# Attention with sinks and a window, then two expert layers: loads, masks and two queues put in a written order

## The chip, the cores and the metric

The kernel runs on one core of one Trainium2 chip. The time is the device time of one execution in microseconds, median of several runs. The engines of the core work side by side, each through its own list of instructions: PE (TensorE), DVE (VectorE), ACT (ScalarE), POOL (GpSimd) and SP (SyncE, which here only issues transfers and holds a queue of its own).

## The reference

Two batches of 8 heads, 768 positions, head size 64. Each position attends to the first `n_sink` = 4 positions and to the last `window` = 128. The result goes to a layer of 8 experts (each token to one of them, by the largest gate logit), and then through a dense layer with the activation h * tanh(softplus(h)).

```python
scores = (q @ k.T) / sqrt(64)
keep   = (pos_k < n_sink) | ((0 <= pos_q - pos_k) & (pos_q - pos_k < window))
a      = softmax(where(keep, scores, -1e9))
x      = (a @ v)                       # 1536 tokens x 512
e      = argmax(x @ w_gate)            # one expert for each token
y      = gate * sigmoid(x @ w_output_gate)[e] * (relu(x @ w1[e]) @ w2[e])
h      = y @ w_in
out    = (h * tanh(softplus(h))) @ w_out
```

`n_sink` and `window` are inputs of the kernel (64-bit integers on the device), and so are the weights w_in and w_out (64-bit floats, read as pairs of 32-bit words and narrowed on the chip).

## The kernel before

There are two forms of attention. `fast()` holds for sinks up to 16 and windows up to 129, which these inputs fulfil; `general()` holds for all others and is not executed here, though its instructions lie in the program between the opening part and the fast form. Every engine reads a flag (`values_load`, L800) and branches (L801).

The opening part loads the two parameters, k and q of the pairs 0 and 1, and prepares constants: masks `m0`, `m1` and `m2` on GpSimd (L194 to L206), which then loads the first 16 rows of v of all heads into `vsr` (L211).

The fast form works on pairs of heads, 8 in all (4 for each batch). A loop over `g` (L641) runs the stages of several pairs in each turn: the scores of pair g, the preparation (transposes of k and q) of pair g + 1, the transposes of the probabilities of pair g - 1, and the product with v and the tail of pair g - 2. In a turn the string in `SEQS` names the order of the parts: p is a quarter of the preparation, s the scores of one block of 128 queries for both heads, a the transposes of the probabilities, v the product, t the tail (transposes back, logits of the gates), m and n copies of the sink columns and the sums, r a part of the routing of a batch whose pairs are done, u a part of the narrowing of w_in. PE keeps this order in any case (`tc.issue_after`). The lists of DVE, ACT, POOL and SP are ordered by a planner, which takes first what it holds to be ready, so the order on them isn't that of the source.

Transfers of a turn, after its parts: `load_kq(g + 3)` (k and q in halves, 8 transfers of 96 KB), `load_v(g + 1)` (2 of 192 KB), one piece of the first expert's weights (512 KB), one or two fills of `table` with zeros (384 KB each, the first 640 KB). QK has two sets of buffers, so a k or q half can only be loaded when the transposes of the pair two before have read it.

Narrowing of w_in: a piece `nr` of 512 KB is loaded (`load_in`, L308), scaled (L294 on GpSimd for pieces below 5, L291 on DVE for others), put together in three steps on DVE (L285, L286, L287) and stored to `wi32` (L318, 256 KB); the store's part also asks for the piece after the next. Seven pieces are done here, piece u in turn u + 2. The loads of the first two pieces stand at the end of turn 0 in the source.

Scores (L547, L549): DVE adds the mask, takes the maximum and frees one of 4 PSUM buffers; ACT makes the exponentials. `kT` is copied by DVE (L510), `qT` by ACT (L512), the sink columns of kT by DVE (L516) for the pairs 0 and 1 and by POOL for others. The product's two banks are copied by DVE (L624, L627); they share 4 PSUM buffers `pt` with all transposes.

Routing (turn 6 for the first batch, turn 10 for the second): `choose` finds the expert of each token, `rank` counts ranks on PE and DVE and gives the row of each token in `table`, and also the factor `gsc` from the gates by way of an exponential `ez` on ACT (L442, L448, L450, L452); `place` scales the rows (L393) and scatters them (L394).

Of the kernel before, what the change touches and what calls it, by code (L numbers as in the profile page):

```python
# [47 lines left out]
def tile_kernel(  # L48
# [21 lines left out]
    keeps = dram.tile([S, S], F32, name="keeps")  # L70
# [32 lines left out]
    def load_kq(g, engs=(nc.sync, nc.sync)):  # L103
        for h in range(2):
            for t, src, eng in zip(QK[g % 2][h], (k, q), engs):
                load_rows(t, src, g, h * LT_, LT_, eng)
# [4 lines left out]
    load_kq(0, (nc.sync, nc.scalar))  # L111
    load_kq(1)
# [26 lines left out]
    ns, wd = pv[:, 0:1], pv[:, 1:2]  # L139
    wx = mid.tile([P, NP, 2, 2 * E], F32, name="wx")  # L140
# [53 lines left out]
    with tc.manual_schedule(engines={ET.Pool}):  # L194
        wdm = mid.tile([P, 1], F32, name="wdm")
# [206 lines left out]
    def route_units(b, sb, pst):  # L402
# [22 lines left out]
        def rank():  # L425
# [36 lines left out]
        def rank_(b=b):  # L462
# [6 lines left out]
        return [choose, rank_] + ([lambda i=i: place(b, 2 * i, 2) for i in range(3)] if b == 0 else [])  # L469
# [15 lines left out]


    def fast():
# [147 lines left out]

        prep0 = prep_units(0)
        for u in prep0[:2]:
            u()
        late, after, tail, routing, prod = [], [], [], [], []
        steps_ = [lambda: None]  # L640
        for g in range(NG + 3):  # L641
# [15 lines left out]
            if g == 0:  # L657
                lane["0"] = [prep0[2], lambda: (prep0[3](), load_kq(2), load_v(0), load_wx())]
# [19 lines left out]
            if g == 0:  # L678
                for u in range(2):
                    load_in(u, nra)  # L680
# [6 lines left out]
            for e in {1: (0,), 2: (1, 2), 3: (3, 4), 4: (5, 6), 5: (7,)}.get(g, ()):  # L687
                zero_fill(e)
        st.close()


    def general():
# [11 lines left out]
        for u in range(2):  # L704
            load_in(u, nra)
        for u in range(NF_):
            for x_ in narrow_in(u, nra, qkv):
                x_()
        rel = cb.tile([P, S], F32, name="grel")
        sk = cb.tile([P, S], F32, name="gsk")  # L710
        nc.gpsimd.iota(rel, [[1, S]], base=0, channel_multiplier=0, allow_small_or_imprecise_dtypes=True)
        nc.vector.tensor_scalar(sk, rel, ns, None, ALU.is_lt)
        g0 = cb.tile([P, S], F32, name="gg0")
        gk = cb.tile([P, S], F32, name="ggk")
        for i in range(NB):
            nc.gpsimd.iota(rel, [[-1, S]], base=i * P, channel_multiplier=1, allow_small_or_imprecise_dtypes=True)
            nc.vector.tensor_scalar(g0, rel, 0.0, None, ALU.is_ge)
            nc.vector.scalar_tensor_tensor(g0, rel, wd, g0, ALU.is_lt, ALU.mult)
            nc.vector.tensor_tensor(gk, g0, sk, ALU.max)
            nc.sync.dma_start(out=keeps[i * P:(i + 1) * P, :], in_=gk)  # L720
# [15 lines left out]
        with tc.For_i(0, B, 1) as b_, tc.For_i(0, NP, 1) as hp, tc.For_i(0, NB, 1) as i:  # L736
            row = b_ * (H * S) + hp * (2 * S)
            for j in range(2):
                cs = slice(j * D, (j + 1) * D)
                nc.sync.dma_start(out=qr[:, cs], in_=qf[ds(row + i * P + j * S, P), :])  # L740
                for t, src in ((kr, kf), (vr, vf)):
                    nc.sync.dma_start(out=t[:, :, cs], in_=src[ds(row + j * S, S), :].rearrange("(i p) d -> p i d", p=P))
                for c_, w_ in ((0, w_gate), (E, w_og)):
                    nc.sync.dma_start(out=wl[cs, j, c_:c_ + E], in_=w_[ds(hp * P + j * D, D), :])
            nc.sync.dma_start(out=keep, in_=keeps[ds(i * P, P), :])
# [4 lines left out]
            for i0 in (0, 3):  # L750
                pt = psT.tile([P, 512], F32, name="pt")
                for a in range(3):
                    nc.tensor.transpose(pt[:, a * P:(a + 1) * P], kr[:, i0 + a], ident)
                nc.scalar.activation(kT[:, i0 * P:(i0 + 3) * P], pt[:, 0:3 * P], AF.Copy)
# [28 lines left out]
            nc.sync.dma_start(out=parts[ds(b_ * (NP * S) + hp * S + i * P, P), :], in_=xo)  # L783
# [832 lines left out]
```

## Time and profile before

| | |
|---|---|
| median of 3 runs | 586.36 us (586.34 to 587.57) |
| the profiled execution | 586.35 us, of which its span 584.7 us |
| PE busy | 557.9 us, 95% of the span |
| DVE busy | 309.2 us, 53% |
| ACT busy | 348.2 us, 60% |
| POOL busy | 46.5 us, 8% |
| DMA | 79.32 MB, mean 136 GB/s |

The span runs from the first instruction to the last. Attention takes about the first 131 us of it, a first chunk of expert 0 goes to 151, the experts go on to 314, and the dense layer fills the rest. A busy share is a mean over stages with different limits.

### The profile page before, as it was taken

How to read it: one execution, taken by the hardware profiler on the slowest of the kernel's cores; microseconds unless marked ns; L12 is line 12 of the kernel's file. 1: busy time of each engine (PE TensorE's matmuls, PEld its weight loads, DVE VectorE, ACT ScalarE, POOL GpSimd, SP SyncE). 2: the span in 40 equal slices, each digit the busy share in tenths (PEclk: the TensorE clock that was granted, in tenths of full speed). 3: DMA queues.
4: the chain of work that ended last, by engine and by line, in shares of the span. 5: the costliest groups of instructions: out<-in, count | busy, mean ns of one | idle time of the engine just before them, and what ended most of it. 6: DMA issues, size and time to landing. Idle time of an engine off the chain costs nothing.

```text
span 584.7 us, 9722 instructions
## 1 busy us (share of the span) xinstructions
PE 557.9 (95%) x3568; PEld 487.5 (83%) x3568; DVE 309.2 (53%) x743; ACT 348.2 (60%) x668; POOL 46.5 (8%) x95
## 2 busy tenths in 40 slices
PE   3859998999999999999999999999999999999995
PEld 2648777789999999999999888888888888888884
DVE  3645788864142036788977996866313233213112
ACT  2837787731111145764546988879767668667572
POOL 8020113204000000000000000000200000200002
PEclk9979999999999999999999999999999999999998
DMA  6697997704999962995421333220100000100002
GB/s 123 145 250 208 235 235 254 242 21 170 377 369 368 324 222 74 399 306 170 126 73 34 102 105 121 72 74 0 73 0 1 0 2 1 73 0 1 0 1 76
DMA packets 72669, 79.32 MB, mean 136 GB/s; under 512 B 42112, under 2 KB 52352, under 8 KB 72608
## 3 DMA queue, kind: packets, MB, share of 16 engines
q1 hardware_dynamic: 68688, 71.61, 40.4%
q0 software_dynamic: 2176, 6.56, 3.0%
q8 instruction: 31, 0.51, 0.4%
q10 hardware_dynamic: 1744, 0.39, 0.4%
q14 instruction: 30, 0.25, 0.1%
HBM read 66.23 MB, written 12.32 MB: 134 GB/s over the span
## 4 chain that ended last, share of the span: by engine, by line
PE 77%; issue 14%; ACT 3%; DMA 2%; DVE 2%; POOL 1%; SPq 0%; POOLq 0%; DVEq 0%; ACTq 0%
PE h L1380 16%; PE acc L1397 15%; PE Y L1067 6%; PE h L1057 6%; PE pt L360 5%; PE Y L1018 5%; PE pt L363 5%; PE h L1000 5%; PE s L363 4%; PE h L1003 3%; ACT p L549 2%; PE Y L1020 2%; PE Y L857 2%; PE h L363 2%; DMA nr<-in_moe_w_in_dram 1%
## 5 line engine op out<-in xcount | busy, mean ns | idle before, releaser
L1429 DVE TENSOR_TENSOR fx<-h,fx 128x512 f32<-128x512 f32 x48 | 30.9, 685 | 127.2 <-ACT fx L1426 127.2
L1420 ACT ACTIVATE fx<-h,nln 128x512 f32<-128x512 f32 x48 | 32.7, 689 | 52.5 <-PE h L1380 52.1
L549 ACT ACTIVATE p<-ms,nm 128x272 f32<-128x272 f32 (+1 forms) x96 | 47.0, 491 | 20.8 <-DVE nm L547 20.8
L1018 PE MATMUL Y<-hs,wch 128*128 128x384 f32 (+1 forms) x160 | 45.3, 355 | 0.0
L1411 POOL DMA_INDIRECT out_dram<-nr,idx x12 | 11.6, 970 | 417.5 <-DVE nr L1407 414.8
L1060 ACT ACTIVATE t<-h 128x256 f32<-128x256 f32 x20 | 7.7, 383 | 58.7 <-PE h L1057 55.0
L547 DVE CUSTOM_DVE_ANT_0 ms<-s,m 128x272 f32<-128x272 f32 (+1 forms) x96 | 34.5, 409 | 11.7 <-ACT ph L579 5.8
L1020 PE MATMUL Y<-hs,wcl 128*128 128x192 f32 (+1 forms) x160 | 39.2, 245 | 0.0
L363 PE MATMUL s<-kT,qT 64*128 64x272 f32 (+1 forms) x192 | 30.2, 418 | 9.2 <-DVE nm L547 6.3
L1380 PE MATMUL h<-yh,wah 128*128 128x512 f32 x96 | 37.5, 391 | 0.0
L1380 PE MATMUL h<-yh,wal 128*128 128x512 f32 x96 | 37.4, 389 | 0.0
L1397 PE MATMUL acc<-wdh,gh 128*128 128x512 f32 x96 | 37.4, 389 | 0.0
L1397 PE MATMUL acc<-wdl,gh 128*128 128x512 f32 x96 | 37.4, 389 | 0.0
L1433 ACT ACTIVATE gh<-fx 128x512 fp32r<-128x512 f32 x48 | 29.5, 633 | 7.2 <-DVE fx L1429 7.2
L1437 DVE TENSOR_TENSOR gl<-fx,gh 128x512 fp32r<-128x512 f32 x48 | 31.0, 688 | 2.4
L1420 ACT ACT_TABLE_LOAD x24 | 30.8, 1283 | 0.4
L1426 ACT ACT_TABLE_LOAD x24 | 30.8, 1283 | 0.4
L1020 PEld LDWEIGHTS Y<-hs,wcl 128*128 128x128 f32 x160 | 30.6, 191 | 0.0
L363 PEld LDWEIGHTS s<-kT,qT 64*128 64x128 f32 x192 | 17.4, 198 | 15.5 <-DVE nm L547 7.3
L1018 PEld LDWEIGHTS Y<-hs,wch 128*128 128x128 f32 x160 | 30.1, 188 | 0.1
L1426 ACT ACTIVATE fx<-fx 128x512 f32<-128x512 f32 x48 | 27.7, 625 | 0.3
L1397 PE MATMUL acc<-wdh,gl 128*128 128x512 f32 x96 | 27.7, 390 | 0.0
(297 smaller groups left out, 1397.6 us busy)
## 6 DMA issues: line engine op xcount, KB each, us to landing
raw<-in_moe_w_dram SPq DMA_DIRECT2D x24, 512.0 KB, 6.6
rbx<-in_moe_w_dram SPq DMA_DIRECT2D x24, 512.0 KB, 6.8
rax<-in_moe_w_dram SPq DMA_DIRECT2D x16, 512.0 KB, 8.3
nr<-in_moe_w_out_dram SPq DMA_DIRECT2D x16, 512.0 KB, 3.8
nr<-in_moe_w_in_dram SPq DMA_DIRECT2D x13, 512.0 KB, 6.4
vr<-in_v_dram SPq DMA_DIRECT2D x16, 192.0 KB, 3.4
table<-zer SPq DMA_DIRECT2D x7, 384.0 KB, 6.6
rax<-wi SPq DMA_DIRECT2D x5, 512.0 KB, 8.4
```

Source lines behind the costliest of these rows:

```text
L363: last_pe[0] = nc.tensor.matmul(*args, **kw)
L547: nc.vector.tensor_tensor_reduce(ms[:, 0:w], s[j][:, 0:w], m, 1.0, 3.0e38, ALU.add, ALU.min, nm[:, j, i:i + 1])
L549: nc.scalar.activation(p[:, j, i, o:o + w], ms[:, 0:w], AF.Exp, bias=nm[:, j, i:i + 1], scale=-1.0, accum_out=sm[:, j, i:i + 1])
L1018: nc.tensor.matmul(Y[c // 2][:, c % 2, 0:2 * w], lhsT=wh, rhs=hT[b][:, f].rearrange("p s c -> p (s c)"), start=(b == 0 and f == 0), stop=F ...
L1020: nc.tensor.matmul(Y[c // 2][:, c % 2, 0:w], lhsT=wl, rhs=hT[b][:, f, 0], start=False, stop=(b == 3 and f == 1), skip_group_check=True)
L1057: nc.tensor.matmul(hp[:, f, 0:P], lhsT=w_[:, d, f * P:(f + 1) * P], rhs=XT[:, d], start=(d == 0), stop=(d == NP - 1), skip_group_check=True)
L1067: nc.tensor.matmul(Y[c // 2][:, c % 2, 0:P], lhsT=raw_[4 + b][:, f * 512 + c * P:f * 512 + (c + 1) * P], rhs=hT[b][:, f, 0:P], start=(b == ...
L1380: mm = nc.tensor.matmul(h, lhsT=wt[:, (fb % 8) * P:(fb % 8 + 1) * P], rhs=xx[d], start=(k_ == 0), stop=(k_ == 11))
L1397: nc.tensor.matmul(accs[tb], lhsT=g_[:, tb * P:(tb + 1) * P], rhs=w_[:, c], start=(fb == 0 and k_ == 0), stop=(fb == NF - 1 and k_ == 2))
L1420: st[n]["sg"] = nc.scalar.activation(x_, st[n]["h"], AF.Sigmoid, bias=nln2)
L1426: nc.scalar.activation(st[n]["x"], st[n]["x"], AF.Sin, scale=2.0)
L1437: nc.vector.tensor_tensor(gl, st[n]["x"], st[n]["gh"].bitcast(F32), ALU.subtract)
```

## The change

In the fast form: SP and DVE are put in source order (`manual_schedule` over the loop). The q halves of pair 1's first part are loaded by ScalarE. The two first loads of w_in move from the end of turn 0 into its part 0, behind `load_kq(2)` and ahead of `load_v(0)`; `load_wx` (four small loads of gate weights) moves the other way, to the end of turn 0. The five operations that make `m1` and `m2` go from GpSimd to DVE, behind the first quarter of the preparation, and `wdm` is made by DVE in the opening part. In `rank` the three operations on `ez` and `se` become a part `weigh`: for the first batch it runs with the first `place`, for the second it stands in one block ahead of `rowf`.

In the general form: one loop over pairs and one over blocks in place of three nested loops, keys and values loaded once for a pair, masks made inside, the gate weights joined in `gates`, and w_in narrowed in larger pieces.

```diff
-    load_kq(0, (nc.sync, nc.scalar))
-    load_kq(1)
+    load_kq(0, (0, 1))
+    load_kq(1, (0,))
...
+    wdm = mid.tile([P, 1], F32, name="wdm")
+    nc.vector.tensor_scalar(wdm, wd, -float(P), None, ALU.add)
...
-        v_.tensor_scalar(wdm, wd, -float(P), None, ALU.add)
-        v_.tensor_scalar(m2[:, 0:P], rel, wdm, BIG, ALU.is_ge, ALU.mult)
-        v_.tensor_tensor(m1[:, 0:P], m2[:, 0:P], sk, ALU.mult)
-        v_.memset(m1[:, P:KW], BIG)
-        v_.tensor_copy(m1[:, KW:WIN], m2[:, KW:WIN])
-        v_.tensor_scalar(m2[:, P:KW], sk[:, 0:SC], BIG, None, ALU.mult)
...
-            nc.vector.tensor_scalar(ez, ez, 1.0, None, ALU.add)
+            if b:
+                weigh()
             nc.vector.tensor_reduce(rowf[:, b], rt, AX.X, ALU.add)
-            nc.vector.scalar_tensor_tensor(se, se, 1e-9, ez, ALU.add, ALU.mult)
             nc.vector.tensor_copy(rowi[:, b], rowf[:, b])
-            nc.vector.reciprocal(gsc[:, b], se)
...
+        def weigh():
+            se, ez = d["se"], d["ez"]
+            nc.vector.tensor_scalar(ez, ez, 1.0, None, ALU.add)
+            nc.vector.scalar_tensor_tensor(se, se, 1e-9, ez, ALU.add, ALU.mult)
+            nc.vector.reciprocal(gsc[:, b], se)
...
-        return [choose, rank_] + ([lambda i=i: place(b, 2 * i, 2) for i in range(3)] if b == 0 else [])
+        return [choose, rank_] + ([lambda: (weigh(), place(b, 0, 2))] + [
+            lambda i=i: place(b, 2 * i, 2) for i in (1, 2)] if b == 0 else [])
...
+    def masks():
+        v_ = nc.vector
+        v_.tensor_scalar(m2[:, 0:P], rel, wdm, BIG, ALU.is_ge, ALU.mult)
+        v_.tensor_tensor(m1[:, 0:P], m2[:, 0:P], sk, ALU.mult)
+        v_.memset(m1[:, P:KW], BIG)
+        v_.tensor_copy(m1[:, KW:WIN], m2[:, KW:WIN])
+        v_.tensor_scalar(m2[:, P:KW], sk[:, 0:SC], BIG, None, ALU.mult)
...
+        order = ExitStack()
+        order.enter_context(tc.manual_schedule(engines={ET.SP, ET.DVE}))
         prep0 = prep_units(0)
         for u in prep0[:2]:
             u()
+        masks()
...
-                lane["0"] = [prep0[2], lambda: (prep0[3](), load_kq(2), load_v(0), load_wx())]
+                lane["0"] = [prep0[2], lambda: (prep0[3](), load_kq(2), load_in(0, nra), load_in(1, nra), load_v(0))]
...
             if g == 0:
-                for u in range(2):
-                    load_in(u, nra)
+                load_wx()
```

The loops of the general form, cut to their heads:

```diff
-        with tc.For_i(0, B, 1) as b_, tc.For_i(0, NP, 1) as hp, tc.For_i(0, NB, 1) as i:
...
+        with tc.For_i(0, B * NP, 1) as g:
+            nc.vector.tensor_copy(rel, rel0)
...
+            with tc.For_i(0, NB, 1) as i:
+                block(g, i)
```

## Rows read from the trace of the kernel before

**Rows 1.** Busy time (instructions) by stretch; last columns: clock, DMA share, GB/s

```profile
core 0: us, PE busy (x) PEld busy (x) DVE busy (x) ACT busy (x) POOL busy (x), PEclk, DMA share, GB/s
15.00:28.00 13.00, 11.65 (x86) 8.03 (x82) 9.10 (x44) 11.90 (x42) 0.63 (x3) 1.00 0.66 142
131.00:584.70 453.70, 446.83 (x2623) 400.45 (x2622) 220.56 (x397) 264.49 (x396) 18.01 (x19) 1.00 0.36 120
```

**Rows 2.** Waits of PE, 0 to 131 us: total, times, longest

```profile
PE s L363 <- DVE nm L547: 6.3, 1, 6.3
...
PE s L363 <- DVE kT L510: 2.9, 1, 2.9
PE pt L360 <- DVE xT L624: 1.7, 2, 1.4
...
PE pt L360 <- DMA q0r<-in_q_dram: 0.6, 2, 0.4
```

**Rows 3.** Chain that ended last, 27 to 38 us: start, duration, what

```profile
29.09 5.93 DMA nr<-in_moe_w_in_dram
...
35.09 1.05 POOL nt L294
```

**Rows 4.** Order of time on DVE, 27.8 to 37.4 us: start, duration, instruction, idle before

```profile
36.17 0.43 DVE L285 TENSOR_SCALAR nt<-nt 128x512 int32<-128x512 int32 x1 [7.83 <-POOL nt L294]
...
37.34 0.78 DVE L286 SCALAR_TENSOR_TENSOR nt<-nr,nt 128x512 int32<-128x512 int32 x1
```

**Rows 5.** Busy time by step of one pair, columns as in rows 1

```profile
27.49:49.72 22.23, 15.53 (x114) 11.79 (x113) 11.07 (x39) 11.28 (x37) 3.26 (x4) 0.85 0.85 214
49.72:62.23 12.51, 12.51 (x115) 10.06 (x114) 7.92 (x33) 10.10 (x33) 0.56 (x2) 1.00 0.98 261
62.23:75.20 12.97, 12.73 (x116) 10.05 (x114) 10.22 (x36) 10.21 (x33) 1.57 (x3) 1.00 0.91 233
...
87.99:102.66 14.67, 13.15 (x127) 10.45 (x125) 12.94 (x60) 10.33 (x35) 5.24 (x7) 1.00 0.80 259
102.66:114.26 11.60, 11.60 (x103) 9.20 (x101) 11.28 (x41) 9.23 (x31) 2.95 (x4) 1.00 0.73 215
```

**Rows 6.** Busy time in the stretch of the lower clock, columns as in rows 1

```profile
35.38:42.20 6.82, 5.19 (x26) 3.78 (x28) 5.54 (x19) 3.80 (x13) 2.97 (x4) 0.50 0.94 217
```

**Rows 7.** Order of time on SP: start, duration of the issues, transfer

```profile
9.32 1.02 SPq L94 DMA_DIRECT2D q1r<-in_q_dram  x2
14.15 0.38 SPq L94 DMA_DIRECT2D vr<-in_v_dram  x1
...
29.09 1.01 SPq L308 DMA_DIRECT2D nr<-in_moe_w_in_dram  x2
```

**Rows 8.** DMA issues from 29, from 30.2 and from 22.35: KB, us to landing

```profile
nr<-in_moe_w_in_dram SPq DMA_DIRECT2D x2, 512.0 KB, 6.4
...
k0r<-in_k_dram SPq DMA_DIRECT2D x2, 96.0 KB, 6.5
...
k0r<-in_k_dram SPq DMA_DIRECT2D x2, 96.0 KB, 3.7
```

**Rows 9.** Order of time on DVE, 91.9 to 104.7 us

```profile
93.73 0.17 DVE L448 TENSOR_SCALAR ez<-ez 128x6 f32<-128x6 f32 x1 [1.44 <-ACT ez L442]
...
94.36 0.88 DVE L393 TENSOR_SCALAR xs<-X,gsc 128x512 f32<-128x512 f32 x2
...
98.73 0.43 DVE L547 CUSTOM_DVE_ANT_0 ms<-s,m 128x272 f32<-128x272 f32 x1
...
103.17 0.43 DVE L547 CUSTOM_DVE_ANT_0 ms<-s,m 128x272 f32<-128x272 f32 x1
```

**Rows 10.** Order of time on PE, the product of step 6

```profile
91.55 2.60 PE L363 MATMUL pt<-ph,vr 128*64 128x256 f32 x28
```

**Rows 11.** Order of time on DVE and ACT behind the branch

```profile
9.66 0.56 DVE L510 COPY kT<-pt 128x384 f32<-128x384 f32 x1 [4.37 <-issue]
...
11.28 0.29 DVE L547 CUSTOM_DVE_ANT_0 ms<-s,m 128x128 f32<-128x128 f32 x1 [0.75 <-PE s L363]
...
7.50 0.49 ACT L512 ACTIVATE qT<-pt 128x384 f32<-128x384 f32 x1 [1.69 <-PE pt L360]
```

More of the change, by code (lines that the diff above doesn't have):

```diff
@@ L69, in tile_kernel @@
     table = dram.tile([E * CAP, DM], F32, name="table")
-    keeps = dram.tile([S, S], F32, name="keeps")
+    gates = dram.tile([B * DM, 2 * E], F32, name="gates")
     parts = dram.tile([B * NB * NP * P, 2 * HC], F32, name="parts")
@@ L101, in tile_kernel, with load_kq @@
     HS = [flat[a_] for a_ in range(5)]
-    def load_kq(g, engs=(nc.sync, nc.sync)):
+    def load_kq(g, on_act=()):
         for h in range(2):
-            for t, src, eng in zip(QK[g % 2][h], (k, q), engs):
+            for t, src, eng in zip(QK[g % 2][h], (k, q), (nc.sync, nc.scalar if h in on_act else nc.sync)):
                 load_rows(t, src, g, h * LT_, LT_, eng)
@@ L194, in tile_kernel @@
     with tc.manual_schedule(engines={ET.Pool}):
-        wdm = mid.tile([P, 1], F32, name="wdm")
         v_.tensor_scalar(sk, col, ns, None, ALU.is_ge)
@@ L460, in rank, with rank_ @@
                 nc.vector.tensor_tensor(left, tot, early, ALU.subtract)
-        def rank_(b=b):
+        def weigh():
[3 more added lines that the diff above has]
+            nc.vector.reciprocal(gsc[:, b], se)
+        def rank_():
             if b:
@@ L688, in fast @@
                 zero_fill(e)
+        order.close()
         st.close()
@@ L703, in general @@
             zero_fill(p_)
[L704 to L707, printed above, removed]
-                x_()
-        rel = cb.tile([P, S], F32, name="grel")
+        for b in range(B):
+            for c_, w_ in ((0, w_gate), (E, w_og)):
+                nc.sync.dma_start(out=gates[b * DM:(b + 1) * DM, c_:c_ + E], in_=w_)
+        nar = cb.tile([P, 2048, 2], I32, name="gnar")
+        nat_ = cb.tile([P, 2048], F32, name="gnat")
+        for d in range(2):
+            cut = w_in32[2 * d * P:(2 * d + 2) * P, 0:2048].rearrange("(a p) f -> p a f", p=P)
+            nc.sync.dma_start(out=nar.rearrange("p f w -> p (f w)").rearrange("p (a f) -> p a f", a=2), in_=cut)
+            for x_ in narrow_steps(nat_, nar, scale_dve):
+                x_()
+            nc.sync.dma_start(out=wi32[2 * d * P:(2 * d + 2) * P, 0:1024].rearrange("(a p) f -> p a f", p=P),
+                              in_=nat_.rearrange("p (a f) -> p a f", a=2))
+        rel0 = cb.tile([P, S], F32, name="grel")
         sk = cb.tile([P, S], F32, name="gsk")
[L711 to L720, printed above, removed]
+        nc.gpsimd.iota(rel0, [[1, S]], base=0, channel_multiplier=0, allow_small_or_imprecise_dtypes=True)
+        nc.vector.tensor_scalar(sk, rel0, ns, None, ALU.is_lt)
+        nc.gpsimd.iota(rel0, [[-1, S]], base=-P, channel_multiplier=1, allow_small_or_imprecise_dtypes=True)
+        rel = cb.tile([P, S], F32, name="grl")
         wl = cb.tile([P, 2, 2 * E], F32, name="gwl")
@@ L734, in general, with block @@
         qf, kf, vf = [x_.rearrange("b h s d -> (b h s) d") for x_ in (q, k, v)]
-        with tc.For_i(0, B, 1) as b_, tc.For_i(0, NP, 1) as hp, tc.For_i(0, NB, 1) as i:
-            row = b_ * (H * S) + hp * (2 * S)
+        def block(g, i):
             for j in range(2):
[L739 to L745, printed above, removed]
+                nc.sync.dma_start(out=qr[:, j * D:(j + 1) * D], in_=qf[ds(g * (2 * S) + i * P + j * S, P), :])
+            nc.vector.tensor_scalar(rel, rel, float(P), None, ALU.add)
+            nc.vector.tensor_scalar(km, rel, 0.0, None, ALU.is_ge)
+            nc.vector.scalar_tensor_tensor(km, rel, wd, km, ALU.is_lt, ALU.mult)
+            nc.vector.tensor_tensor(keep, km, sk, ALU.max)
             nc.vector.tensor_scalar(km, keep, BIG, -BIG, ALU.mult, ALU.add)
@@ L749, in general @@
             nc.scalar.activation(qT, pt[:, 0:P], AF.Copy, scale=0.125)
[L750 to L754, printed above, removed]
             for j in range(2):
@@ L782, in general @@
             nc.vector.tensor_copy(xo, pt[:, 0:2 * HC])
-            nc.sync.dma_start(out=parts[ds(b_ * (NP * S) + hp * S + i * P, P), :], in_=xo)
+            nc.sync.dma_start(out=parts[ds(g * S + i * P, P), :], in_=xo)
+        with tc.For_i(0, B * NP, 1) as g:
+            nc.vector.tensor_copy(rel, rel0)
+            for j in range(2):
+                cs = slice(j * D, (j + 1) * D)
+                for t, src in ((kr, kf), (vr, vf)):
+                    nc.sync.dma_start(out=t[:, :, cs],
+                                      in_=src[ds(g * (2 * S) + j * S, S), :].rearrange("(i p) d -> p i d", p=P))
+                nc.sync.dma_start(out=wl[cs, j, :], in_=gates[ds(g * P + j * D, D), :])
+            for i0 in (0, 3):
+                pt = psT.tile([P, 512], F32, name="pt")
+                for a in range(3):
+                    nc.tensor.transpose(pt[:, a * P:(a + 1) * P], kr[:, i0 + a], ident)
+                nc.scalar.activation(kT[:, i0 * P:(i0 + 3) * P], pt[:, 0:3 * P], AF.Copy)
+            with tc.For_i(0, NB, 1) as i:
+                block(g, i)
         for b in range(B):
```

## The prediction

> **What bounds the kernel now.** I read the waits of the matrix engine first, then the chain of waits, then the queues that feed the point it leads to. Only the attention part is touched by what runs: the general form is jumped over with these inputs, so the expert and MLP parts move as a block with the end of attention. From 131 us on PE is busy almost without a gap [rows 1], so a microsecond won or lost before 131 is a microsecond of the total.
>
> PE waits for little in attention: 6.3 us once for DVE's maxima of the scores, 2.9 us once for the first kT copy, 1.7 us in two pieces for the copy of xT [rows 2]. The large one is in the chain [rows 3]: the load of the first w_in piece `nr` lands 5.93 us after its issue, GpSimd scales it (1.05 us), and only then does DVE go on. DVE's own rows [rows 4] show why PE cares: L285, the first DVE step on that piece, stands on DVE ahead of the score rows (L547) of the same pair step, and waits there 7.83 us. PE fills its score buffers and stops.
>
> Cut into steps (a step is a turn of the loop on PE, from its first k transpose to that of the next turn), turn 2, from 27.49 to 49.72, lasts 22.23 us where the next two last 12.51 and 12.97 [rows 5]. Part of it is the clock: the granted clock reads 0.50, the lower of the two levels, over the 6.82 us after the stall, with 5.19 us of PE work in it [rows 6]; at the full level this work takes half, so about 2.6 us. Stall 6.3 and clock 2.6 make 8.9 of the 9.7 us by which the step is longer than the next one.
>
> Why was the piece late? SyncE issued it at 29.09, behind 24 other loads sent from 14.15 on, at about 0.5 us each [rows 7]. The order was the scheduler's.
>
> **The change, part by part.**
>
> *First w_in loads.* In source order SyncE sends, after its jump, the 8 loads of pair 2's k and q, then both `nr` pieces, then v. It also has 2 loads fewer before the jump (two of pair 1's q move to ScalarE). SP's last issue ahead of the jump ended at 10.34, and two issues took 1.02 us there [rows 7], so the jump comes 1 to 2 us earlier and the first load of the fast form goes out between 12.1 and 14.15. Eight issues at 0.5 us put `nr` at 16 to 18.3 instead of 29.09; with the 6.4 us it took to land under load [rows 8] it is there by 22.5 to 24.7. What is pushed behind it, pair 3's k and q, took 3.7 us to land alone and 6.5 us behind `nr` [rows 8]: issued by about 18.5 to 22.5, there by 25 to 29. Pair 3's k is needed at 27.49, so a wait of 0 to 1 us can stay; one of 0.4 us is there already, and I count no difference.
>
> *DVE in source order.* L285 and L286 of a piece come after the product of the step, not before its scores, in steps 2, 3, 4 and so on, one piece a step. Step 2 then looks like its neighbours: 22.23 down to about 12.6, **-9.6 us** (bounds: -6.3, if the clock falls all the same, and -9.8). Steps 3 to 5 are PE-bound with DVE busy 7.9 to 10.2 us of 12.5 to 13 [rows 5]: I take 0, with +-0.5.
>
> Do later pieces arrive in time? A step carries 3.3 MB (k, q and v 1.18, one weight piece 0.52, two zero fills 0.79, one `wi32` store 0.26, one `nr` 0.52); at the 261 GB/s of the step at a DMA share of 0.98 [rows 5] this is 12.6 us, just a step. The queue does not drain, but a piece is asked for about 2 us into the step before the one that uses it, with some 2.1 MB (8 us) ahead, and DVE wants it 5.5 us into its own: 14 to 16 us against 10. I count 0 and keep the shortfall as a rival.
>
> *Step 6, the first batch's routing.* Here DVE is the bound: 12.94 us busy of 14.67, and 11.28 of 11.60 in the next [rows 5]. Before, DVE waited 1.44 us at L448 for ScalarE's exp ahead of the xT copy, and PE waited 1.44 for that copy [rows 9, 2]. The change puts `weigh` and the first two rows of `place` behind the product and the ranks, so that wait goes. But the scheduler had filled gaps with pieces that source order puts in one row. After the product (PE ends it near 94.2 [rows 10]) I count on DVE: the rest of the xT copies to 94.7; twelve rank operations, 2.0 (0.17 each, a little more where one waits for another [rows 9]); L285 and L286, 1.2 [rows 4]; one kT copy, 0.55; `weigh` and two `place` rows, 0.6 + 0.9 [rows 9]. That is 5.2, so the next scores are read at 99.9 instead of 98.73 [rows 9]. To the scores after these come, in source order, `sums` (0.4) and a fourth `place` row (0.45) that had been done earlier: 105.5 instead of 103.17. PE's scores of step 7 wait for these buffers, and a part of 2.3 us may fall into small waits that PE has there already: I take **+1.9 us**; bounds -1.4 (the PE wait of 1.44 goes and DVE catches up) and +3.
>
> *Masks.* Five operations leave GpSimd and stand on DVE between L516 and the first scores, with `wdm` further ahead. Four are 16 to 128 columns wide, between the 0.17 of a 6-column row [rows 9] and the 0.43 of a 512-column one [rows 4]: with the memset about 1.0 us, 0.7 to 1.8. DVE idled 0.75 us there [rows 11], so +0.25 (0 to 1). GpSimd's loads of v for the sinks start earlier by as much as it is spared, which nobody waits for.
>
> *Loads of k and q 2 earlier, q on ScalarE.* SP starts up to 2 us sooner, and PE waited 0.6 us for such loads [rows 2]; but ScalarE leads there, busy 11.9 of 13 us [rows 1]. Two issues at 0.5 us on ScalarE ahead of its jump may hold the first qT copy, which had 2 us of room because kT came last [rows 11]. Together -0.25, which cancels the masks; bounds -0.6 and +0.8.
>
> *Last routing.* `weigh` now stands as a block ahead of rowf: three dependent operations of 0.17 to 0.19 that had been interleaved, so rows and scatter come about **+0.2** later; at worst 0.5, at best nothing, since PE computes through it.
>
> *Gates, keeps and the two loops* of the general form are not executed: 0, unless through the place of the code (rival 2).
>
> **Sum.** -9.6 + 0 + 1.9 + 0 + 0.2 = -7.5. The profiled execution has a span of 584.7 and a time of 586.35, and the median of the runs is 586.36, so no correction: about **578.8 us**. A measurement of this kernel can tell some 0.2% (1.2 us) from no change.
>
> **A jump and its price.** DVE's first operation behind the branch starts 4.37 us after its last one ahead of it, and the row names no releaser ("issue") [rows 11], though the transposes it copies had been followed by those of q, which ScalarE took up at 7.50. SP has a gap of the same kind, 10.34 to 14.15 [rows 7]. I take both as staying, since the fast form still lies behind the general one: 0 in the sum. The Trainium skill (Runtime: NRT & Kernel Launch, section Instruction fetch mechanics) says that a taken branch stalls only if its target is outside the current two-page window; the idle rows agree with such a stall. By that rule a general form with less code could bring the target inside, which is rival 2.
>
> **Rivals.**
> 1. *DVE is not the bound in step 6.* For it: DVE lost 1.44 us there that it need not lose. Against: 11 to 13 us of DVE work in each of two steps. Then -1.4 in place of +1.9: 575.5.
> 2. *The jump gets short.* Without DVE's idle time kT is copied near 7; ScalarE's qT copy, 7.50 to 8.0 [rows 11], then sets the scores at 8.1 instead of 10.3, behind the kT copy of 9.66 to 10.2: -2.2, 576.6. For it: less DVE code to jump over. Against: nothing shows where the window ends.
> 3. *DMA becomes the bound of steps 2 to 5.* At the 233 GB/s of the step from 62.23 [rows 5] instead of 261, 3.3 MB take 14.2 us, 1.6 more than a step, over three steps about +5: 584. For it: shares of 0.98 and 0.91. Against: PE did not wait for a load there, and a piece has 4 to 6 us of room.
> 4. *Slower: the stall comes back in every step.* In source order a late piece stops DVE at L285 and PE behind it. If each of the pieces 2 to 5 came over 2 us late, four stalls eat the 7.5 us; at 3 us each (and the clock's fall with it) 592. It decides if a piece lands later than 18 us after its request; it took 6.4 [rows 8], so about 3 MB more would have to stand ahead of it.
> 5. *The stall only moves.* `nr` comes early, but k and q of pair 3 come late by as much: PE waits at 27.5 instead of 30.7, and the time is 585 to 587. Against: SP has 10 us more than before.
>
> **Chances.** Forecast 0.52; rival 1 0.18; rival 2 0.10; rival 3 0.10; rival 4 0.05; rival 5 0.05. The predicted time is the likeliest, 578.8. The range holds the forecast with its own bounds (step 6 and step 2 each off by 2) and rivals 1 and 2: 574.5 to 583.5. Rival 3 just falls out. Faster: forecast, rivals 1 to 3, 0.90. Same: rival 5, 0.05. Slower: rival 4, 0.05.
>
> **What would show it.** DVE's wait at L285 for nt is gone and L285 follows L624 and L627 in each step; `nr` is issued by SP near 17; the step at 27 lasts 12.5 to 13 and the granted clock stays 1.00 in it. In step 6 the PE wait for xT is gone but PE waits for L547 near the start of step 7 (in the new time about 9 us earlier). If L285 still waits over 1 us for GpSimd, or PE for k0r or q0r, the first term is wrong; if steps 6 and 7 together take 26.3 us or less, the third is; if DVE's first kT copy starts near 7, rival 2 holds.

## The result and the profile after

| | before | after |
|---|---|---|
| time, median (range) of 4 runs each on one chip | 586.91 (586.34 to 587.57) | 581.37 (580.18 to 582.19) |
| ratio after to before, 95% interval | | 0.9904 (0.9881 to 0.9927) |
| span of the profiled execution | 584.7 | 579.6 |
| last turn of attention ends, first expert matmul `pt<-vr,raw` on PE | 128.40 | 123.18 |

The change is faster by 5.5 us; the forecast was 7.5 less than before. All of it was won ahead of the first expert matmul: from there to the end both spans need 456 us. So the reading goes by turn. Below, the view of busy time by stretch of the kernel after, one row for turn 1 to turn 5, one for turns 6 and 7 with what follows up to the expert part; it answers to [rows 5], with the columns of [rows 1].

```profile
core 0: us, PE busy (x) PEld busy (x) DVE busy (x) ACT busy (x) POOL busy (x), PEclk, DMA share, GB/s
12.68:28.02 15.34, 12.23 (x81) 8.70 (x79) 8.21 (x40) 12.14 (x42) 2.52 (x4) 0.89 0.87 205
28.02:41.02 13.00, 12.57 (x116) 10.06 (x114) 9.41 (x36) 10.82 (x36) 0.56 (x2) 1.00 0.78 188
41.02:53.53 12.51, 12.51 (x116) 10.06 (x114) 9.42 (x36) 10.04 (x33) 0.56 (x2) 1.00 0.92 244
53.53:66.07 12.54, 12.54 (x115) 10.06 (x114) 9.48 (x35) 10.10 (x33) 1.60 (x3) 1.00 0.87 228
66.07:79.58 13.51, 13.01 (x116) 10.34 (x114) 10.36 (x38) 10.10 (x33) 1.60 (x3) 1.00 0.84 225
79.58:123.18 43.60, 40.42 (x368) 32.29 (x366) 34.12 (x123) 25.79 (x83) 8.44 (x11) 0.96 0.64 197
```

Set against before:

| part | before | after | difference | forecast |
|---|---|---|---|---|
| start to turn 1 | 15.27 | 12.68 | -2.6 | 0 |
| turn 1 | 12.22 | 15.34 | +3.1 | 0 |
| turns 2 to 5 | 60.50 | 51.56 | -8.9 | -9.6 |
| turns 6, 7 and what follows, to the expert part | 40.41 | 43.60 | +3.2 | +2.1 |
| sum | 128.40 | 123.18 | -5.2 | -7.5 |

Turn 2 lost its stall and its low clock as forecast. Two things came that the sum did not hold: the kernel gets through its branch sooner, and it gives that back in turn 1.

**The front.** The next rows are the order of time on VectorE behind the branch, after; they answer to [rows 11]. The first kT copy comes at 6.43 instead of 9.66, and its idle time now ends with PE, not with "issue".

```profile
4.89 0.15 DVE L142 TENSOR_SCALAR wdm<-pv 128x1 f32<-128x1 f32 x1
6.43 0.56 DVE L520 COPY kT<-pt 128x384 f32<-128x384 f32 x1 [1.38 <-PE pt L356]
...
7.14 0.48 DVE L491 TENSOR_SCALAR m<-rel,wdm 128x128 f32<-128x128 f32 x1
...
8.71 0.29 DVE L557 CUSTOM_DVE_ANT_0 ms<-s,m 128x128 f32<-128x128 f32 x1 [0.26 <-PE s L359]
```

The masks, which stand behind two of the four quarters of the preparation, fit: five operations between 7.14 and 8.45, and the first score rows then wait 0.26 us for PE, not for a mask. SyncE's order of time answers to [rows 7]: its first load behind the branch goes out at 11.02 instead of 14.15, and the piece `nr` at 15.50 instead of 29.09.

```profile
11.02 1.25 SPq L94 DMA_DIRECT2D k0r<-in_k_dram  x2
...
15.50 0.96 SPq L304 DMA_DIRECT2D nr<-in_moe_w_in_dram  x2
...
17.62 3.45 SPq L94 DMA_DIRECT2D k0r<-in_k_dram  x2
```

**A new wait in turn 1.** The waits of PE answer to [rows 2]: the 6.3 us for the maxima is gone, as is the 1.7 for xT, and two others stand there.

```profile
PE pt L356 <- POOL pk L568: 2.3, 1, 2.3
PE s L359 <- DVE nm L557: 2.2, 1, 2.2
```

The first is explained by the chain that ended last (start, duration, what), which answers to [rows 3]: the same load and the same scale on GpSimd, now 13.6 and 14.9 us earlier, and behind them a copy of sink columns, `pk`, that has nothing to do with the piece.

```profile
15.50 4.66 DMA nr<-in_moe_w_in_dram
20.17 0.07 issue
20.24 1.04 POOL nt L290
21.28 0.24 POOL pk L568
21.52 0.05 issue
21.57 2.58 PE pt L356 x15
```

GpSimd's own order shows that it stood: the scale of the piece had been put ahead of `pk` and waited 7.75 us for the load. When `pk` could have run is shown by the run with `pk` first below (17.36, when ScalarE's exponentials are there).

```profile
20.24 1.04 POOL L290 TENSOR_TENSOR nt<-nr,tiny 128x512 f32<-128x512 f32 x1 [7.75 <-DMA nr<-in_moe_w_in_dram]
21.22 0.29 POOL L568 COPY pk<-p 128x128 f32<-128x128 f32 x1
```

**The clock.** PE's busy time in four stretches, after, as [rows 6] for before: the two waits, and the stretch shortly behind each in which the granted clock is 0.50, the lower level.

```profile
core 0: us, PE busy (x), PEclk, DMA share, GB/s
19.27:21.57 2.30, 0.00 (x1) 1.00 1.09 326
22.54:25.95 3.41, 3.41 (x17) 0.50 0.74 147
94.86:97.08 2.22, 0.00 (x1) 1.00 0.56 212
97.63:101.05 3.42, 3.42 (x18) 0.50 0.91 223
```

PE is busy throughout both low stretches, so at the full level the same work would take half: 1.7 us lost in each.

**Turn 6.** VectorE's order of time there answers to [rows 9]: behind the xT copy the ranks, the steps on `nt`, the kT copy, `weigh` and two rows of `place`, all ahead of the score rows.

```profile
86.30 0.42 DVE L637 COPY xT<-pt 128x256 f32<-128x256 f32 x1 [0.20 <-PE pt L359]
...
88.57 0.42 DVE L281 TENSOR_SCALAR nt<-nt 128x512 int32<-128x512 int32 x1
...
90.73 0.88 DVE L389 TENSOR_SCALAR xs<-X,gsc 128x512 f32<-128x512 f32 x2
91.53 0.43 DVE L557 CUSTOM_DVE_ANT_0 ms<-s,m 128x272 f32<-128x272 f32 x1
...
96.58 0.43 DVE L557 CUSTOM_DVE_ANT_0 ms<-s,m 128x272 f32<-128x272 f32 x1
```

From the end of the xT copies (86.72) to the scores it is 4.8 us, where the forecast counted 5.2, and 5.05 to the next ones, where it counted 5.6. The count was good; what it costs PE was sized too small. The cost falls into turn 7: turn 6 lasts 14.22 us against 14.67 before, turn 7 15.23 against 11.60, and what follows 14.15 against 14.14. First the busy time of turn 6 (columns of [rows 1]), then, from PE's order of time, the last scores of turn 6, which took 1.19 us before:

```profile
79.58:93.80 14.22, 13.93 (x128) 10.83 (x126) 12.16 (x57) 9.30 (x32) 3.58 (x5) 1.00 1.02 308
```

```profile
92.10 1.74 PE L359 MATMUL s<-kT,qT 64*128 64x272 f32 x8
```

### The profile page after: what moved, and what is told of

Same layout as the page of the kernel before. It is cut to its first block, busy times and chain, and to the rows that moved or that the text cites. A ratio compares the mean times of both kernels' runs of the same rounds, so it can differ in the third digit from the quotient of the medians.

```text
span 579.6 us, 9743 instructions
## 1 busy us (share of the span) xinstructions
PE 558.7 (96%) x3568; PEld 488.4 (84%) x3568; DVE 311.6 (54%) x749; ACT 348.2 (60%) x668; POOL 43.9 (8%) x89
## 4 chain that ended last, share of the span: by engine, by line
PE 79%; issue 14%; ACT 2%; DMA 1%; POOL 1%; DVE 1%; POOLq 0%; SPq 0%; DVEq 0%; ACTq 0%
PE h L1402 16%; PE acc L1419 15%; PE Y L1089 6%; PE pt L359 6%; PE h L1079 6%; PE pt L356 6%; PE Y L1040 5%; PE h L1022 5%; PE s L359 4%; PE h L1025 3%; PE Y L1042 2%; PE Y L879 2%; PE h L359 2%; ACT p L559 1%; POOL out_dram L1433 1%
## 5 line engine op out<-in xcount | busy, mean ns | idle before, releaser
L1402 PE MATMUL h<-yh,wal 128*128 128x512 f32 x96 | 37.4, 389 | 0.0
L1419 PE MATMUL acc<-wdl,gh 128*128 128x512 f32 x96 | 37.4, 389 | 0.0
L1419 PE MATMUL acc<-wdh,gh 128*128 128x512 f32 x96 | 37.4, 389 | 0.0
L589 ACT ACTIVATE ph<-pt 128x512 f32<-128x512 f32 (+1 forms) x48 | 24.9, 556 | 7.0 <-PE pt L356 4.2
```

The lines of the kernel that those rows point to most:

```text
L1402: mm = nc.tensor.matmul(h, lhsT=wt[:, (fb % 8) * P:(fb % 8 + 1) * P], rhs=xx[d], start=(k_ == 0), stop=(k_ == 11))
L1419: nc.tensor.matmul(accs[tb], lhsT=g_[:, tb * P:(tb + 1) * P], rhs=w_[:, c], start=(fb == 0 and k_ == 0), stop=(fb == NF - 1 and k_ == 2))
```

## The experiments

Two theories had to be told apart for turn 2: that the piece's late load was the cause (then an earlier load is enough), and that VectorE's order was. For the front: that the shorter code made the jump short, or the edits around it. For turns 1, 6 and 7: that the two new waits cost what they seem to, or that another bound stands behind them. All ratios are against the kernel before, run on the same chip; its median lay between 586.82 and 587.22 in the other sets of runs. Two parts of the change have no run of their own: the q loads on ScalarE, and `weigh`.

| kernel | median us | ratio (95%) | turn 2 starts | turns 6, 7 and rest |
|---|---|---|---|---|
| before | 586.91 | 1 | 27.49 | 40.41 |
| after | 581.37 | 0.9904 (0.9881 to 0.9927) | 28.02 | 43.60 |
| early loads alone | 586.72 | 0.9997 (0.9986 to 1.0007) | 35.62 | 41.56 |
| new general form alone | 585.34 | 0.9969 (0.9954 to 0.9984) | 25.05 | 41.68 |
| after, old general form | 583.37 | 0.9931 (0.9911 to 0.9952) | 28.69 | 44.69 |
| after, no source order | 585.05 | 0.9974 (0.9963 to 0.9985) | 32.35 | 41.63 |
| after, source order on SyncE only | 580.95 | 0.9897 (0.9877 to 0.9918) | 29.23 | 42.16 |
| after, source order on VectorE only | 581.56 | 0.9902 (0.9876 to 0.9928) | 26.16 | 45.17 |
| after, loads at the old place | 579.77 | 0.9887 (0.9861 to 0.9912) | 24.52 | 43.65 |
| after, masks on GpSimd | 582.36 | 0.9939 (0.9914 to 0.9964) | 27.66 | 44.68 |
| after, pk first on GpSimd | 580.01 | 0.9877 (0.9849 to 0.9904) | 24.98 | 44.90 |
| after, two place steps in turn 7 | 579.22 | 0.9864 (0.9834 to 0.9895) | 27.93 | 40.68 |
| pk first and place steps moved | 576.71 | 0.9828 (0.9800 to 0.9855) | 25.39 | 40.75 |
| loads at the old place and place steps moved | 576.73 | 0.9834 (0.9814 to 0.9854) | 24.93 | 40.76 |

### Early loads alone

```
-lane["0"] = [prep0[2], lambda: (prep0[3](), load_kq(2), load_v(0), load_wx())]
+lane["0"] = [prep0[2], lambda: (prep0[3](), load_kq(2), load_in(0, nra), load_in(1, nra), load_v(0))]
...
-                for u in range(2):
-                    load_in(u, nra)
+                load_wx()
```

> The kernel before, with the two early loads of w_in pieces issued behind the loads of k and q of pair 2 and the gate weights at the end of turn 0, and nothing else; the scheduler's order stays on SyncE and VectorE. Theory A (the late load was the whole cause of the stall in turn 2): the piece is issued by SyncE before 20 us, VectorE's wait at L285 falls from 7.83 to under 1 us, turn 2 lasts 12.5 to 14 us and the time falls by 6 to 9 us, to 578 to 581. Rival B (the source order is needed, since the scheduler goes on by its own estimate of the load and issues it late whatever the source says): the piece goes out near 29 us again, L285 waits 5 us or more and the time is within 1.2 us of the kernel before.

Neither. The scheduler did send the piece early, at 13.71, ahead even of pair 2's k. But it also moved VectorE's step on it forward, into turn 0. VectorE's order of time shows the stall of [rows 4] again, 16.7 us earlier and as long:

```profile
11.65 0.28 DVE L547 CUSTOM_DVE_ANT_0 ms<-s,m 128x128 f32<-128x128 f32 x1
...
19.50 0.43 DVE L285 TENSOR_SCALAR nt<-nt 128x512 int32<-128x512 int32 x1 [7.55 <-POOL nt L294]
```

PE stops 7.3 us behind it (the view of waits names ScalarE's qT copy, which itself stands behind the exponentials of VectorE's late score rows), and the granted clock is low for 10.24 us from 17.43 on.

```profile
PE s L363 <- ACT qT L512: 7.3, 1, 7.3
```

A load that comes sooner is worth nothing as long as the step behind it moves forward with it.

### The table of four: source order on SyncE, on VectorE, on both, on neither

VectorE only:

```
-order.enter_context(tc.manual_schedule(engines={ET.SP, ET.DVE}))
+order.enter_context(tc.manual_schedule(engines={ET.DVE}))
```

With `{ET.SP}` in its place it is SyncE only, and without the line neither.

> The kernel after with only VectorE in source order; SyncE's order is the scheduler's again. Theory (VectorE's order carries the gain in turn 2 and the loss in turns 6 and 7; the source now places the piece's load behind pair 2's loads, and the scheduler moves it by little): no wait over 1 us of VectorE for a piece in turn 2, turn 2 lasts 12.5 to 14 us, turns 6 and 7 together 43 to 44 us; the time is within 1.5 us of the kernel after, 580 to 583. Rival (SyncE's order is needed, the scheduler issues the piece near 29 us again): VectorE waits for it behind the product of turn 2, from about 33 to 37, turn 2 lasts over 15 us and the time is 584 or more.

The theory held in turn 2 and in the time: VectorE never waits for a piece, turn 2 lasts 13.28 us and the time is that of the kernel after. It missed twice: the scheduler moved the load far, to the first place behind SyncE's branch, at 11.36, and turns 6, 7 and the rest last 45.17 us instead of the 43 to 44 said, with a low stretch of 6.83 us in turn 7.

> The kernel after with only SyncE in source order; VectorE's order is the scheduler's again. Theory (the load's place alone does not help; VectorE's order is what removes the stall): VectorE's first step on a w_in piece stands ahead of score rows of turn 1 and waits 5 to 8 us for the piece, PE stops 5 us or more before turn 2, and the time is 3 to 7 us above the kernel after, 584 to 588; turns 6 and 7 get shorter by about 3 us, which is in that figure. Rival (with the piece early on SyncE the scheduler places the step behind its landing): no wait over 1 us on VectorE, turns 6 and 7 3 us shorter, and the time 2 to 3 us below the kernel after, about 578.5.

Neither: the time is that of the kernel after. VectorE does wait for the piece ahead of score rows, but in turn 1 and for half as long:

```profile
21.68 0.48 DVE L281 TENSOR_SCALAR nt<-nt 128x512 int32<-128x512 int32 x1 [3.38 <-POOL nt L290]
```

PE stands for `pk` in that time in any case (1.9 us), so little is added. Turns 6 and 7 are 1.4 us shorter than after, with no low clock in them.

> The kernel after with the scheduler's order on SyncE and on VectorE (neither in source order); with the kernel after, the one with only SyncE and the one with only VectorE in source order it makes a table of four. Theory (what the source order does is to keep VectorE from standing at a piece of which the load is not there; either order alone was enough, neither is not): VectorE's first step on a piece stands ahead of score rows of turn 1 and waits 3 to 7 us, PE stops 3 us or more in turns 1 or 2, and the time is 583 to 587. Rival (the new place of the load and the short jump are all that was needed): no PE wait over 2.5 us behind 6 us, and the time is 579.5 to 582.

The theory held, 585.05, though the stall comes a turn earlier than it said. With neither order fixed VectorE stands at the piece in turn 0 already, behind its first two score rows, and PE for 6.2 us behind it (again by way of ScalarE's qT copy). The first block shows VectorE's order of time, the second a line of the waits of PE:

```profile
10.15 0.29 DVE L557 CUSTOM_DVE_ANT_0 ms<-s,m 128x128 f32<-128x128 f32 x1
...
16.70 0.43 DVE L281 TENSOR_SCALAR nt<-nt 128x512 int32<-128x512 int32 x1 [6.25 <-POOL nt L290]
```

```profile
PE s L359 <- ACT qT L522: 6.2, 1, 6.2
```

PE also waits 2.0 us for the first kT copy, which the scheduler puts behind masks; with SyncE only it does the same, so this isn't what parts the two.

So the source order is worth 3.7 us by the medians beside the rest of the change, and either engine's is enough. In the profiled executions it is 2.4: turn 2 starts 4.3 us later without it, and 2.0 come back in turns 6 and 7, where source order costs time. On VectorE it acts directly. Why the scheduler puts VectorE's step later when SyncE is fixed is not shown; it may go by when it thinks the load is there.

### The jump

The kernel after with the general form of before, cut to its core; the other kernel is the kernel before with the reverse of this:

```
-    gates = dram.tile([B * DM, 2 * E], F32, name="gates")
+    keeps = dram.tile([S, S], F32, name="keeps")
...
-        with tc.For_i(0, B * NP, 1) as g:
+        with tc.For_i(0, B, 1) as b_, tc.For_i(0, NP, 1) as hp, tc.For_i(0, NB, 1) as i:
```

> The kernel after with the general form of before (one loop over three counters, mask written to memory): nothing of what runs is changed, only the code that is jumped over is longer. Theory (the shorter code is what made the jump short): VectorE's first kT copy starts near 9 to 10 us instead of 6.43, SyncE's gap at its branch is near 3 us instead of 0.5, PE's first scores wait some 2 us longer; the time rises by 0 to 2.5 us against the kernel after, nearer 0 if the later wait of PE on pk at 19 to 21.6 us absorbs it. Rival (the jump got short because the edits around it changed what SyncE and VectorE do ahead of it): the first kT copy stays near 6.4 us and the time is the same within 0.5 us.

> The kernel before with the general form of after (two loops, mask made inside) and nothing else: code that is jumped over gets shorter, what runs stays. Theory (the length of the skipped code sets the idle time behind the branch, and the edit to it is worth some 2 us by itself): VectorE's first kT copy starts at 6.4 to 7.0 us instead of 9.66, SyncE's first load behind its branch at about 11.3 instead of 14.15; as SyncE reaches the w_in piece some 2.8 us sooner, the stall of turn 2 moves with the front and keeps its size, and the time falls by 1.5 to 2.8 us, to about 584.5. Rival (the gain of the short jump seen in the changed kernel needs the other edits ahead of the branch): kT copy near 9.7, time the same within 0.6 us.

Both theories held, the second at the lower edge of its range. In the kernel after with the old general form, VectorE and SyncE are late behind the branch again (order of time on both):

```profile
9.60 0.56 DVE L520 COPY kT<-pt 128x384 f32<-128x384 f32 x1 [4.57 <-issue]
...
13.47 1.14 SPq L94 DMA_DIRECT2D k0r<-in_k_dram  x2
```

and in the kernel before with the new one both are early:

```profile
6.44 0.56 DVE L510 COPY kT<-pt 128x384 f32<-128x384 f32 x1 [1.56 <-PE pt L360]
...
11.34 0.37 SPq L94 DMA_DIRECT2D vr<-in_v_dram  x1
```

Nothing but code that never runs differs within each pair, and the order of operations on each engine is the same. It is worth 2.0 us in the one (581.37 to 583.37; the runs do not overlap, the intervals against before do) and 1.5 in the other (586.82 to 585.34, on that chip). In the second the front is 2.4 us ahead at turn 2 and 1.3 are lost behind turn 5: nearly all of it is one wait of PE, 1.18 us at 102.12 for ScalarE's copy `ph`, which the kernel before doesn't have; what delays `ph` stays open. ScalarE and GpSimd take the same branch and show nothing of the kind: with the old and the new general form in the kernel after, their next instruction comes 0.67 and 0.20 us behind it in both. The edit changes both how much code is skipped and where the target lies, so that it is the length which counts is argued, not shown.

### The load's place, with source order kept

```
-lane["0"] = [prep0[2], lambda: (prep0[3](), load_kq(2), load_in(0, nra), load_in(1, nra), load_v(0))]
+lane["0"] = [prep0[2], lambda: (prep0[3](), load_kq(2), load_v(0), load_wx())]
...
-                load_wx()
+                for u in range(2):
+                    load_in(u, nra)
```

> The kernel after with the two early loads of w_in pieces back at the end of turn 0, behind v and the gate weights, and both engines in source order. Theory A (the piece is asked for only in turn 2 behind the product, near 35 us, so a load some 4 us later still comes in time, and it lets pair 3's k and q pass): the piece is issued near 19.5 to 21 us, VectorE does not wait for it over 1 us, turn 2 lasts 12.5 to 13.5, and the time is within 1 us of the kernel after, or 1 to 3 us less if GpSimd's scale falls behind pk for that reason. Rival B (the new place carries the gain): GpSimd's scale still stands ahead of pk, the PE wait on pk grows from 2.3 to 5 us or more, and the time is 583 to 586.

Theory A: the time falls by 1.6 us by the medians (the intervals overlap), though the piece goes out later than it said, at 26.26 by SyncE's order of time:

```profile
26.26 1.01 SPq L304 DMA_DIRECT2D nr<-in_moe_w_in_dram  x2
```

That is 2.8 us ahead of [rows 7], and still the stall is gone: VectorE asks for the piece behind the product and waits 1.9 us (the theory allowed 1), and the waits of PE have none on it. GpSimd does `pk` first, and turn 2 starts at 24.52. Turns 2 and 3 are longer than after, 13.91 and 13.77 against 13.00 and 12.51, and turn 2 longer than the theory's 12.5 to 13.5; what lengthens them is open. From the waits of VectorE:

```profile
DVE nt L281 <- POOL nt L290: 1.9, 1, 1.9
```

### Masks

```
+        v_.tensor_scalar(m2[:, 0:P], rel, wdm, BIG, ALU.is_ge, ALU.mult)
...
+        v_.tensor_scalar(m2[:, P:KW], sk[:, 0:SC], BIG, None, ALU.mult)
...
-        masks()
```

> The kernel after with the five mask operations back on GpSimd. Theory (with the short jump the scores are ready at 8.6 us, and GpSimd, which is at 8.07 behind its first masks, needs 1.6 to 2 us for the other five): VectorE's first score rows start at 9.7 to 10.2 us instead of 8.71; the 1.0 to 1.5 us are swallowed by the wait on pk, which ends with the piece's load, so turn 2 starts within 0.6 us of 28.0 and the time is within 0.8 us of the kernel after. Rival (the front's delay goes through to the end, or GpSimd's loads of v for the sinks, now later, hold PE): time 1 to 2.5 us above the kernel after.

Inconclusive on the time, and the mechanism was not as I had it: the first score rows, at 8.68, need none of the moved masks; the next ones wait 0.44 us for GpSimd and start 0.12 us later than after. Turn 2 starts 0.36 us earlier than after. The 1.0 us by which the time is above after lies in turns 6 and 7, where the low stretch lasts 6.83 us instead of 3.42. The masks' place is worth nothing that I can show.

### The two new waits

Pk first:

```
+        with tc.issue_after(last_pk[-1].ins) if last_pk else ExitStack():
+            nc.gpsimd.tensor_tensor(o, i, tiny.to_broadcast([P, 512]), ALU.mult)
...
-                nc.gpsimd.tensor_copy(pk, p[:, :, 2:NB, P:KW].rearrange("p j i c -> p i j c"))
+                last_pk.append(nc.gpsimd.tensor_copy(pk, p[:, :, 2:NB, P:KW].rearrange("p j i c -> p i j c")))
```

Two place steps in turn 7:

```
-        6: "mruppassvruaprassntrtaurpss",
-        7: "muppassvuapassnttaupss",
+        6: "mruppassvruaprassnttaupss",
+        7: "muppassvuarpassnttaurpss",
...
+            if g == 6:
+                routing = lane["r"][3:]
+                del lane["r"][3:]
```

> The kernel after, with one edit: GpSimd's scale of a w_in piece is issued behind the latest copy pk of the sink columns. Theory (the changed kernel lost 2.3 us of PE to GpSimd's order, as the scale stood ahead of pk and waited 7.75 us for its load, and 1.7 us more to the clock at its lower level): the PE wait of 2.30 us on pk is gone, pk is done before 14 us, the granted clock stays 1.00 between 22 and 26 us, turn 2 starts between 24.0 and 25.5 us instead of 28.02, and the time falls by 2.5 to 4 us against the kernel after, to 577.4 to 579. Rival (the front of the attention is bound by the loads of pair 3, which stand in SyncE's queue behind the early piece): PE waits for k0r or q0r instead, turn 2 starts later than 26.5, and the time falls by less than 1 us.

The place was right: no wait for `pk`, no low clock there, turn 2 starts 3.0 us earlier. Two sizes were not: `pk` runs at 17.36, when ScalarE's exponentials are there, and not before 14; and only 1.4 us reach the median, where 2.5 to 4 were expected. Busy time by stretch of that kernel, for turn 5, turns 6 and 7, and the low stretch in turn 7 (PE alone):

```profile
63.31:77.41 14.10, 13.50 (x116) 10.64 (x114) 10.96 (x38) 10.14 (x34) 1.60 (x3) 1.00 0.93 264
77.41:122.31 44.90, 41.74 (x368) 33.26 (x366) 34.11 (x123) 25.78 (x83) 8.46 (x11) 0.92 0.61 192
```

```profile
94.75:101.58 6.83, 6.68 (x38) 0.50 0.93 297
```

Behind the same 2.22 us wait for VectorE the clock stays low for 6.83 us instead of 3.42: half of the difference, 1.7, covers the 1.3 us that turns 6 and 7 are longer. Turn 5 is 0.6 us longer; in turn 4 VectorE had waited 1.2 us for its piece, and I take it that it is still behind.

> The kernel after, with the second and third place step of the first batch moved from turn 6 to turn 7. Theory (in turn 6 VectorE in source order has more rows in one line than PE's two score buffers cover, so PE waits 2.22 us at L557 and then computes at the lower clock for 3.4 us): the wait near 95 us shrinks to under 0.7, the clock stays 1.00 near 98, turns 6 and 7 together last 2 to 3.9 us less than 43.6 minus what follows them, and the time falls by 2 to 3.9 us, to 577.5 to 579.4. Rival (turns 6 and 7 are bound by the sum of VectorE's work, so what is moved comes back one turn later): PE waits as long at a later score row and the time changes by less than 0.7 us.

Right in place and size; by the intervals against before alone the gain of 2.2 us isn't clear of the kernel after (they overlap), but the trace shows it in its place. The wait shrinks to 0.6 us, no low clock follows, and turns 6 and 7 are 2.9 us shorter. From the waits of PE:

```profile
PE s L359 <- DVE nm L557: 0.6, 1, 0.6
```

> Both edits that helped alone: GpSimd's scale behind pk (it gave back of its 3.0 us in turn 2 0.6 us in turn 5 and 1.3 us in turns 6 and 7), and two place steps moved from turn 6 to turn 7 (2.9 us less in turns 6 and 7). Theory (what the first gave back in turns 6 and 7 was the same VectorE bound, with a longer stretch at the lower clock): the two add up, turn 2 starts near 25, turns 6 and 7 last 40.5 to 41.2 us, the granted clock stays 1.00 near 95, and the time is 576 to 577.5. Rival (the weight pieces, which come by DMA, set the pace from turn 4 on, so an earlier front only waits for them): VectorE waits over 2 us for pieces in turns 4 to 6 and the time is 578.5 to 579.5, as with the place steps alone.

The theory held: they add up, 576.71, with no stretch at the lower clock in turns 2 to 7.

```profile
77.28:118.03 40.75, 39.16 (x368) 31.21 (x366) 34.00 (x123) 25.78 (x83) 8.16 (x11) 1.00 0.64 204
```

This beats both kernels, and its interval (0.9800 to 0.9855) is clear of that of the kernel after.

> The kernel after with the two w_in loads back at their old place in the source and the two place steps moved to turn 7. Both engines stay in source order, and GpSimd's pk does not stand behind the piece, as it did not with the old place alone. Theory (with VectorE in source order the early place of the load gives nothing; it is only what the order on VectorE does that counts): turn 2 starts near 24.5 us, turns 6 and 7 last 40.5 to 41.2 us, no stretch at the lower clock behind 12 us, and the time is 576.3 to 578, within 1 us of the version with the early load, pk first and the place steps moved (576.71). Rival (the early load is worth what turns 2 and 3 lost with the old place, 13.91 and 13.77 us against 13.33 and 12.51): 1.5 to 2.5 us more than that version, 578.2 to 579.2.

The theory held, 576.73 against 576.71: with VectorE in source order and GpSimd not behind the piece, the early place of the load gives nothing that these runs can tell.

## Why the prediction was right, and where it was off

**The stall of turn 2, -9.6 forecast, -8.9 measured in turns 2 to 5.** Right in mechanism and nearly in size. L281 follows the xT copies, the granted clock reads 1.00 in turns 2 to 5. The attribution was shared out wrongly, though. The prediction gave the earlier load and the order on VectorE one term. The runs part them: the load's place alone nothing (0.9997), the source order 3.7 us with everything else in place, and with that order the early place no more than the old one. Taken out of the kernel after one at a time, the order costs 3.7 us and the shorter skipped code 2.0; together 5.7, near the 5.5 of the whole change.

**The jump, 0 in the sum.** The step "I take both as staying" failed; rival 2, held at 0.10, came true in its mechanism: turn 1 starts 2.6 us earlier where it said 2.2. Two runs show that the skipped code does it. The two SyncE loads fewer ahead of the branch, for which the prediction counted 1 to 2 us, give 0.7 (first load behind it at 13.47 with the old general form, at 14.15 before). The Trainium skill (Runtime: NRT & Kernel Launch, section Instruction fetch mechanics) has a taken branch stall when its target lies outside the current two-page window. The two runs agree with the direction of that rule (in the kernel after, VectorE's first instruction comes 4.0 us behind the branch with the old general form and 0.8 with the new); none shows how far the window reaches.

**Front, masks and early loads, 0 forecast.** What stands behind a step on a late piece was asked of VectorE only. GpSimd's order was still the scheduler's, and it put the piece's scale ahead of `pk`, as VectorE's had been ahead of the scores. This is the wait that took the place of the one removed: 2.30 us, and up to 1.7 for the clock behind it, against the 2.6 that the jump gave. Rival 5 had the kind of it (the stall only moves) but looked for it at pair 3's k and q, for which PE does not wait (its one wait for a q half, 0.3 us in turn 1, is for pair 2). The run with `pk` first shows the price, 3.0 us at the start of turn 2.

**Turns 6 and 7, +1.9 and +0.2 forecast, +3.2 measured.** The hand count of VectorE's rows held within 0.6 us. The term was mis-sized in two ways: the wait reached PE whole (2.22) instead of in part, and the 3.42 us at the lower clock behind it had no price, although the first part had priced exactly that for turn 2. With the wait for xT gone (1.44) that makes 2.22 + 1.7 - 1.44 = 2.5, and the longer last scores of turn 6 (1.74 against 1.19) 0.55 more; the other 0.1 is not traced. The +0.2 for the last routing does not show: what follows turn 7 lasts as long as before. Rival 1 is wrong: moving two steps off VectorE's line in turn 6 takes 2.9 us away.

**Rivals 3 and 4.** In the kernel after, DMA does not bind: VectorE waits at most 0.2 us for a piece, DMA share 0.78 to 0.92 in turns 2 to 5. With an earlier front it starts to show: 1.2 us of wait with pk first, 1.9 with the old place. The stall did not come back in every turn.

So the gain fell 2.0 us short of the forecast by the medians (2.3 in the profiled executions): 0.7 in turns 2 to 5, 0.5 in the front, where two unpriced effects of some 3 us nearly cancel, and 1.1 in turns 6 and 7.

## What to carry to other kernels

When a late load stalls an engine, first ask which engines have been given a step on it ahead of other work: moving the load moves the stall, and fixing the order on one engine leaves it to the next whose order a scheduler still makes. Count such a step on every engine, and price each PE wait of 2 us with the low clock that may follow it. And code that is jumped over is not free: here it was worth about 3 us on VectorE and 2.5 on SyncE, and nothing on ScalarE and GpSimd, so look at each engine's first instruction behind the branch.

## What the runs showed of the hardware that was not expected

The record of the granted clock begins between 11 and 15.5 us; ahead of that, where the views print 1.00, the first transposes of three blocks take 0.85 to 0.90 us, as they do within a low stretch (0.90 at 20.27 without source order), against 0.49 to 0.55 later. Within the record the stretches at the lower clock lasted, in attention: 3.41 or 3.42 us (after, twice; loads at the old place; SyncE only; place steps moved; masks on GpSimd in turn 1), 6.82 or 6.83 (before; new general form alone; pk first; old general form; VectorE only; masks on GpSimd in turn 7) and, beginning within turn 0, 6.83 (no source order) and 10.24 (early loads alone). The same 2.2 us wait for VectorE in turn 7 was followed by 3.42 us in the kernel after and by 6.83 with pk first or with the masks on GpSimd, and a 2.0 us wait for `pk` with the old general form by none. So a wait near 2 us cost between nothing and 3.4 us of PE time beyond itself, and kernels that differ only elsewhere differ by 1.7 us through it.

A branch over the general form left VectorE idle 4.37 to 4.97 us with the old code and 1.35 to 1.56 with the new in the kernels where the kT copy comes first, the latter ended by PE; SyncE's next load came 2.8 to 3.1 us behind its branch with the old and 0.5 with the new. ScalarE and GpSimd show no such difference between the two forms.
